# Attention and highway layer on one core: the last sum of the highway layer and the doubling of x on GpSimd in place of VectorE

## The chip, the cores and the metric

One core of one Trainium2 chip runs the whole kernel. The metric is the device time of one execution in microseconds (us); a lower figure is better.

Names of engines: PE is TensorE's matmul, PEld its weight load, DVE is VectorE, ACT is ScalarE, POOL is GpSimd, SP is SyncE.

## The reference

Sliding-window attention (window 128, plus 4 sink keys) over 4 batches, 8 heads, 768 positions, head size 64, then a highway layer over the 3072 tokens with 512 features:

```python
def _attn_ref(q, k, v, n_sink, window):
    scores = scale * np.matmul(q, k.transpose(0, 1, 3, 2))
    scores = np.where(is_sink | in_window, scores, -1e9)
    a = np.exp(scores - scores.max(-1, keepdims=True))
    a = a / (a.sum(-1, keepdims=True) + 1e-09)
    return np.matmul(a, v)
# x = attention's output as [3072, 512]
def _moe_ref(x, w_h, w_t, b_t):
    H = np.maximum(x @ w_h, 0.0)
    T = 1.0 / (1.0 + np.exp(-(x @ w_t + b_t)))
    return T * H + (1.0 - T) * x
```

## The kernel before

The kernel works on 24 tiles of 128 tokens, six per batch (c = 0 to 5). It keeps half of x (xh = x/2) in fp16, so that the gate is T = (1 + tanh)/2 and the output is 2·xh + (1 + u)·dd with u = tanh and dd = max(hps, 0) − xh, where hps is half of x·w_h. The order on PE, DVE and ACT is the program order; GpSimd's order is chosen by the scheduler. All loads of q, k and v are issued by GpSimd, which is busy for about 0.9 us with each (914 ns for q, 916 for k).

```python
    td_pool = ctx.enter_context(tc.tile_pool(name="p_td", bufs=3))     # u, dd, ee
    m_ps = ctx.enter_context(tc.tile_pool(name="ps_m", bufs=2, space=bass.MemoryType.PSUM))
    # ... (cut)
    def stage_T(n):                       # transposes of q and k, for tile n
        tp = m_ps.tile([P, 2 * NHP, P], FP16, tag="m", name="tp")
        # ... 8 transposes on PE (cut)
        nc.scalar.copy(out=qT, in_=tp[:, 0:NHP, :])
        nc.vector.tensor_copy(out=kT, in_=tp[:, NHP:2 * NHP, :])

    def stage_mask(n):                    # two masks a tile; both inputs are in SBUF
        for e in es:
            nc.vector.tensor_tensor(out=ev, in0=ev,
                in1=m.unsqueeze(1).to_broadcast([P, 4, np_ * P]), op=ALU.mult)

    # stage_A ends with rec = 1/sum and xh = av * rec (av is in PSUM), on VectorE
    # stage_sink_setup (once a batch) has two small copies on VectorE (ks), then vs, the sinks' values:
            nc.vector.tensor_copy(out=ks3[rows, :, 4 * hh:4 * hh + NSINK],
                                  in_=kT[rows, :, 0:NSINK])

    def stage_Mh(n):
        # ... 4 matmuls into hps (cut)
        dd = td_pool.tile([P, DM], FP16, tag="dd", name="dd")
        nc.vector.scalar_tensor_tensor(out=dd, in0=hps, scalar=0.0, in1=xh,
                                       op0=ALU.max, op1=ALU.subtract)
        ee = td_pool.tile([P, DM], FP16, tag="ee", name="ee")
        nc.vector.scalar_tensor_tensor(out=ee, in0=u, scalar=1.0, in1=dd,
                                       op0=ALU.add, op1=ALU.mult)
        otok = o_pool.tile([P, DM], FP32, tag="otok", name="otok")
        nc.vector.scalar_tensor_tensor(out=otok, in0=xh, scalar=2.0, in1=ee,
                                       op0=ALU.mult, op1=ALU.add)
        nc.sync.dma_start(out=out[n * P:(n + 1) * P, :], in_=otok)

    with tc.manual_schedule(engines={ENG.PE, ENG.DVE, ENG.Activation}):
        for i in range(-2, NB + 1):
            # load(i+4); sink(i); S(i+1); A(i); T(i+2); mask(i+1); Mt(i-1); X(i); sink setup; Mh(i-1)
```

The softmax here doesn't subtract the row's maximum and nothing guards it: scores larger than these inputs give would overflow.

## Time and profile before

| | kernel before |
|---|---|
| time, median | 144.44 us (144.27 to 144.75) |
| span of the profiled run | 143.0 us |
| six tiles (one batch) in the steady part | 29.1 us |
| from hps to hps: tile with sink scores, without, c = 0, sink setup, the one after it | 5.00, 4.55, 4.50, 5.47, 4.60 us |

The last row is worked out from the start times of the first hps matmul of each tile in the timeline.

Lines of the page of the kernel before. The first is the busy time of each engine, its share of the span and its instructions; the second is the chain of waits that ended last; the others are groups: line, engine, operation, output and inputs with their shapes, count, busy us and mean ns of one, then the idle time before them.

```profile
PE 114.4 (80%) x1312; PEld 73.8 (52%) x1312; DVE 114.1 (80%) x228; ACT 90.3 (63%) x129; POOL 66.8 (47%) x86
...
DVE 36%; PE 32%; ACT 10%; DMA 7%; issue 7%; POOL 6%; DVEq 0%; POOLq 0%
...
L247 DVE TENSOR_TENSOR e<-e,mask 128x1024 f16<-128x1024 f16 x32 | 20.5, 682 | 0.0
...
L316 DVE SCALAR_TENSOR_TENSOR ee<-u,dd 128x512 f16<-128x512 f16 x24 | 16.6, 692 | 2.9 <-ACT es L214 0.5
...
L319 DVE SCALAR_TENSOR_TENSOR otok<-xh,ee 128x512 f32<-128x512 f16 x24 | 16.6, 692 | 0.8
```

VectorE and TensorE are equally busy, and VectorE leads the chain, so an operation taken off VectorE looks like a gain. But the chain alternates between the engines, and one tile of the timeline shows why. Columns: start, duration, engine, line, operation; in brackets the idle time before it and what ended it.

```profile
60.19 0.69 DVE L319 SCALAR_TENSOR_TENSOR otok<-xh,ee 128x512 f32<-128x512 f16 x1
...
60.80 0.20 DVE L275 RECIPROCAL rec<-av 128x8 f32<-128x8 f32 x1
...
61.04 0.69 DVE L277 TENSOR_TENSOR xh<-av,rec 128x512 f16<-128x512 f32 x1
...
61.50 0.58 ACT L176 COPY qT<-tp 128x512 f16<-128x512 f16 x1
...
62.12 0.42 DVE L177 COPY kT<-tp 128x512 f16<-128x512 f16 x1 [0.39 <-ACT qT L176]
...
62.46 1.28 DVE L247 TENSOR_TENSOR e<-e,mask 128x1024 f16<-128x1024 f16 x2
62.60 1.02 PE L310 MATMUL hps<-wh_sb,xT 128*128 128x512 f16 x4
...
63.66 0.69 DVE L313 SCALAR_TENSOR_TENSOR dd<-hps,xh 128x512 f16<-128x512 f32 x1
...
64.46 0.69 DVE L316 SCALAR_TENSOR_TENSOR ee<-u,dd 128x512 f16<-128x512 f16 x1
```

VectorE is ready for kT at 61.73 but waits 0.39 us for ScalarE's qT, and hps starts right after kT. An earlier xh would not have moved this hps. In this kernel "VectorE is 80% busy" and "VectorE's work sets the time" are different statements.

### The profile page before, as it was taken

Reading aid. Unit: us, or ns where it says so; the run is one execution under the profiler, and the core shown is the slowest. Engines: PE = TensorE matmul, PEld = TensorE weight load, DVE = VectorE, ACT = ScalarE, POOL = GpSimd, SP = SyncE. Lnnn points to the kernel's source line nnn. Section 1 sums busy time; section 2 is a strip of 40 time slices with the busy share of each in tenths; the row PEclk is TensorE's granted clock in tenths of the full one; section 3 lists DMA queues with packets and bytes.
Section 4 is the critical chain, followed back from the end, with each engine's and each line's share of the span. In section 5 each row is a group of like instructions: output and inputs, shape, how many; then the busy total and the mean of one; then the engine's idle time right before and its main releaser. Section 6 shows DMA issues by size and latency. Waiting matters only on the chain.

```text
span 143.0 us, 3308 instructions
## 1 busy us (share of the span) xinstructions
PE 114.4 (80%) x1312; PEld 73.8 (52%) x1312; DVE 114.1 (80%) x228; ACT 90.3 (63%) x129; POOL 66.8 (47%) x86
## 2 busy tenths in 40 slices
PE   0345046999999969999999699999997999999730
PEld 0134034775676525756765366567644656675310
DVE  6825007588989899989898999899889998999690
ACT  3056026187787677779766867887759579774310
POOL 6999569719975744376349424753040000000000
PEclk9999999999999999999999999999999999999996
DMA  1999999999999998999999999999869021011111
GB/s 10 112 126 156 161 155 155 155 112 142 150 179 201 163 181 64 155 153 137 131 153 125 160 100 135 146 138 134 113 101 124 0 78 73 14 64 73 73 73 73
DMA packets 79408, 16.98 MB, mean 119 GB/s; under 512 B 75297, under 2 KB 76321, under 8 KB 79394
## 3 DMA queue, kind: packets, MB, share of 16 engines
q0 software_dynamic: 75936, 10.49, 109.1%
q1 hardware_dynamic: 3458, 6.30, 12.7%
q8 instruction: 10, 0.16, 0.4%
q14 instruction: 4, 0.03, 0.1%
HBM read 20.97 MB, written 6.29 MB: 191 GB/s over the span
## 4 chain that ended last, share of the span: by engine, by line
DVE 36%; PE 32%; ACT 10%; DMA 7%; issue 7%; POOL 6%; DVEq 0%; POOLq 0%
PE hps L310 12%; DMA ksd<-in_k_dram 7%; DVE ee L316 6%; DVE otok L319 6%; DVE e L247 6%; DVE dd L313 5%; ACT e L234 5%; DVE xh L277 5%; PE av L262 4%; PE tps L298 4%; PE xtp L286 3%; DVE kT L177 3%; PE sk L211 3%; ACT qT L176 2%; DVE vs L196 2%
## 5 line engine op out<-in xcount | busy, mean ns | idle before, releaser
L234 ACT ACTIVATE e<-sps,ebias 128x1024 f16<-128x1024 f32 (+1 forms) x48 | 47.4, 1039 | 15.7 <-PE sps L231 11.4
L298 PE MATMUL tps<-wt_sb,xT 128*128 128x512 f16 x96 | 25.1, 384 | 0.0
L310 PE MATMUL hps<-wh_sb,xT 128*128 128x512 f16 x96 | 24.6, 378 | 0.6
L83 POOL DMA_DIRECT2D qsd<-in_q_dram x24 | 21.9, 914 | 2.7 <-PE tp L173 1.7
L176 ACT COPY qT<-tp 128x512 f16<-128x512 f16 x24 | 14.0, 585 | 14.1 <-PE tp L173 14.1
L84 POOL DMA_DIRECT2D ksd<-in_k_dram x24 | 22.0, 916 | 2.0 <-DMA wh_sb<-in_moe_w_h_dram 2.0
L262 PEld LDWEIGHTS <-e 128*128 128x128 f16 x352 | 20.4, 100 | 4.2 <-DVE vs L196 1.2
L247 DVE TENSOR_TENSOR e<-e,mask 128x1024 f16<-128x1024 f16 x32 | 20.5, 682 | 0.0
L301 ACT ACTIVATE u<-tps 128x512 f16<-128x512 f32 x24 | 14.4, 600 | 9.0 <-PE tps L298 9.0
L177 DVE COPY kT<-tp 128x512 f16<-128x512 f16 x24 | 10.0, 418 | 12.0 <-ACT qT L176 12.0
L313 DVE SCALAR_TENSOR_TENSOR dd<-hps,xh 128x512 f16<-128x512 f32 x24 | 16.5, 687 | 3.4 <-PE hps L310 3.4
L316 DVE SCALAR_TENSOR_TENSOR ee<-u,dd 128x512 f16<-128x512 f16 x24 | 16.6, 692 | 2.9 <-ACT es L214 0.5
L171 PE MATMUL tp<-ident,qsd 128*128 128x128 f16 x96 | 10.2, 234 | 10.6 <-DMA qsd<-in_q_dram 10.6
L231 PE MATMUL sps<-qT,kT 64*128 64x128 f16 x352 | 15.2, 228 | 2.8 <-DVE kT L177 2.1
L319 DVE SCALAR_TENSOR_TENSOR otok<-xh,ee 128x512 f32<-128x512 f16 x24 | 16.6, 692 | 0.8
L277 DVE TENSOR_TENSOR xh<-av,rec 128x512 f16<-128x512 f32 x24 | 16.6, 691 | 0.8
L231 PEld LDWEIGHTS <-kT 64*128 64x128 f16 x352 | 10.7, 99 | 10.1 <-issue 6.8
L288 ACT COPY xT<-xtp 128x512 f16<-128x512 f16 x24 | 14.0, 583 | 1.2 <-PE xtp L286 0.7
L298 PEld LDWEIGHTS <-xT 128*128 128x128 f16 x96 | 9.6, 100 | 9.1 <-issue 0.8
L310 PEld LDWEIGHTS <-xT 128*128 128x128 f16 x96 | 9.2, 97 | 8.1 <-issue 1.3
L171 PEld LDWEIGHTS <-qsd 128*128 128x128 f16 x96 | 7.4, 104 | 11.2 <-DMA qsd<-in_q_dram 10.8
L286 PEld LDWEIGHTS <-xh 128*128 128x128 f16 x96 | 6.2, 100 | 13.1 <-DVE xh L277 11.5
(66 smaller groups left out, 161.8 us busy)
## 6 DMA issues: line engine op xcount, KB each, us to landing
out_dram<-otok SPq DMA_DIRECT2D x24, 256.0 KB, 2.6
qsd<-in_q_dram POOLq DMA_DIRECT2D x24, 128.0 KB, 4.9
ksd<-in_k_dram POOLq DMA_DIRECT2D x24, 128.0 KB, 5.3
v_91<-in_v_dram POOLq DMA_DIRECT2D x4, 128.0 KB, 4.2
v_92<-in_v_dram POOLq DMA_DIRECT2D x4, 128.0 KB, 3.9
wt_sb<-in_moe_w_t_dram POOLq DMA_DIRECT2D x1, 512.0 KB, 7.4
wh_sb<-in_moe_w_h_dram POOLq DMA_DIRECT2D x1, 512.0 KB, 9.5
v_93<-in_v_dram POOLq DMA_DIRECT2D x4, 128.0 KB, 5.3
```

The costliest lines, as they stand in the source:

```text
L83: nc.gpsimd.dma_start(out=qsd, in_=q[b, :, rows, :].transpose([1, 0, 2]))
L84: nc.gpsimd.dma_start(out=ksd, in_=k[b, :, rows, :].transpose([1, 0, 2]))
L231: nc.tensor.matmul(sps[:, hh, o:o + P], lhsT=kk[rows, hp, :], rhs=qT[rows, hp, :], start=True, stop=True)
L234: nc.scalar.activation(out=e.rearrange("p a b c d -> p a (b c d)"), in_=sps[:, :, 0:2 * np_ * P], func=AF.Exp, bias=ebias, scale=SCALE)
L247: nc.vector.tensor_tensor(out=ev, in0=ev, in1=m.unsqueeze(1).to_broadcast([P, 4, np_ * P]), op=ALU.mult)
L262: nc.tensor.matmul(av[:, g, 2 * hl + hh, 0:_AVN], lhsT=es[g][:, hh, hl, pc, :], rhs=vt[:, 65 * h:65 * h + _AVN], start=first, stop=False, ...
L277: nc.vector.tensor_tensor(out=xh, in0=avh[:, :, 0:D], in1=rec.unsqueeze(2).to_broadcast([P, H, D]), op=ALU.mult)
L298: nc.tensor.matmul(tps, lhsT=xT[:, kc, :], rhs=wt_sb[:, kc, :], start=False, stop=(kc == NOC - 1))
L310: nc.tensor.matmul(hps, lhsT=xT[:, kc, :], rhs=wh_sb[:, kc, :], start=(kc == 0), stop=(kc == NOC - 1))
L313: nc.vector.scalar_tensor_tensor(out=dd, in0=hps, scalar=0.0, in1=xh, op0=ALU.max, op1=ALU.subtract)
L316: nc.vector.scalar_tensor_tensor(out=ee, in0=u, scalar=1.0, in1=dd, op0=ALU.add, op1=ALU.mult)
L319: nc.vector.scalar_tensor_tensor(out=otok, in0=xh, scalar=2.0, in1=ee, op0=ALU.mult, op1=ALU.add)
```

## The change

The intent is to take 24 operations of 0.69 us off VectorE and give them to an engine that is 47% busy. GpSimd gets two operations for each one removed: the doubling of xh, which does not depend on the long chain, and the sum. (VectorE's form does both in one operation. A version with that same scalar_tensor_tensor on GpSimd did not compile.)

```diff
     u_of = {}
+    xh2_of = {}
@@ stage_Mh
+        xh2 = td_pool.tile([P, DM], FP16, tag="xh2", name="xh2")
+        nc.gpsimd.tensor_scalar_mul(xh2, xh, 2.0)
+        xh2_of[n] = xh2
         dd = td_pool.tile([P, DM], FP16, tag="dd", name="dd")
@@
         otok = o_pool.tile([P, DM], FP32, tag="otok", name="otok")
-        nc.vector.scalar_tensor_tensor(out=otok, in0=xh, scalar=2.0, in1=ee,
-                                       op0=ALU.mult, op1=ALU.add)
+        nc.gpsimd.tensor_tensor(out=otok, in0=xh2_of.pop(n), in1=ee, op=ALU.add)
         nc.sync.dma_start(out=out[n * P:(n + 1) * P, :], in_=otok)
```

## The prediction

> **What bounds the kernel now.** The page shows PE 80%, DVE 80%, ACT 63%, POOL 47% busy of a 143.0 us span; the chain of waits gives DVE 36% and PE 32%. So DVE looks like the limit. Read in order of time, the steady part (40 to 127 us, 29.1 us per six token tiles) says something narrower. In most tiles two things end together: DVE's otok, rec, xh, and ScalarE's qT copy; kT needs both, and hps waits for kT. From hps start to hps start a tile without sink scores takes 4.55 us, one with them 5.0 us. Both are rebuilt without otok: hps 0.95, (sk 0.46), 0.49 from scores to exponential, two exponentials 2.01, qT 0.62, kT 0.42, 0.06 to hps. In these tiles qT ends between 0.35 us after xh and 0.08 us before it. Only around a batch's first tile (c = 0, half-size exponentials) is DVE clearly late: xh ends 0.57 us after qT, and 0.18 us in the tile after the sink setup.
>
> **Removed, added, moved.** DVE loses 24 otok operations, 692 ns each by record, about 0.61 us by spacing: 15 to 16.6 us of DVE time. POOL gains 24 scalings and 24 sums. Its own memsets (231 ns for 128 elements, 352 for 256) suggest 0.6 us for the scaling. For the sum the Trainium skill, "GPSIMD Engine Reference", section 3.1, gives 4497 ns for 2048 fp32 elements; my estimate for 512 is 1.2 us. No trace here shows either yet. POOL also issues all loads, three of 0.88 us per tile, so its work per tile goes from 2.65 to 4.45 us while loads last (to about 105 us). The instruction order puts each sum between load issues, so POOL will lag. But loads run five to six tiles ahead, and three ee and xh2 buffers allow two tiles of lag: no stall from POOL's throughput.
>
> **Contention.** The Trainium skill, "SBUF — State Buffer", section "Who interferes with whom", says that a DVE instruction with two SBUF inputs contends with a GpSimd instruction that reads SBUF. Here these are the two masks (682 ns each) and ee (692 ns), against both new POOL operations. The trace of before cannot show this. I estimate 0.3 to 0.6 us of DVE delay per tile, which eats most of the 0.61 us freed.
>
> **On the critical path.** Without contention the gain is about 0.75 us per batch boundary (0.45 at c = 0, the rest in the next two tiles), three boundaries: 2.2 us. At the end xh comes 0.7 and dd 0.6 us earlier, but the last sum takes 0.5 us longer and the last hps must still follow: net 0.2 to 0.4 us. Best case about 142. Contention gives back about 1 us.
>
> **Prediction: 143.0 us, range 141.2 to 145.8.** Chances: faster by over 2% 0.09, within 2% 0.84, slower by over 2% 0.07.
>
> **Right or wrong in the profile.** DVE busy falls by 12 us or more (less if masks and ee lengthen); POOL busy rises by 40 us or more; sums near 1.2 us, scalings 0.6 us; hps to hps still 4.55 and 5.0 us in mid-batch tiles; c = 0 tiles 0.4 us shorter; kT waits for ScalarE in nearly all tiles (five in the steady part before); loads issued later but never waited for by transposes.
>
> **What would make it wrong.** If POOL locks DVE out for whole operations more than once a tile, DVE loses over 0.7 us per tile and the kernel is slower by some us. If fp16 sums take 1.6 us or more, POOL lags until ee waits for buffers. If an earlier xh shortens the ScalarE loop too, the gain could reach 4 us.

## More of the kernel before

A pair of full masks, undisturbed, takes 1.28 us in the timeline.

## The result

The changed kernel took 152.49 us (151.46 to 152.95, four runs) against 144.57 us in the same rounds. The ratio is 1.054, with a 95% interval of 1.048 to 1.060: 5.4% slower, and outside the predicted range. Ratios in this document are the mean time of one kernel's fast runs over the mean of the other's fast runs of the same rounds, so they are not quite the ratio of the medians.

The same lines of the page after:

```profile
PE 116.3 (77%) x1312; PEld 74.1 (49%) x1312; DVE 119.1 (79%) x204; ACT 90.8 (60%) x129; POOL 136.1 (90%) x134
...
DVE 43%; PE 21%; ACT 12%; issue 8%; DMA 6%; POOL 6%; POOLq 1%; DVEq 0%; ACTq 0%
...
L247 DVE TENSOR_TENSOR e<-e,mask 128x1024 f16<-128x1024 f16 x32 | 30.7, 1000 | 0.0
...
L320 DVE SCALAR_TENSOR_TENSOR ee<-u,dd 128x512 f16<-128x512 f16 x24 | 20.6, 858 | 3.1
```

VectorE executes 24 instructions fewer and is busy 5.0 us longer. The 16.6 us of otok went, and 21.3 us came back: 13 us on full masks (25.6 to 38.7 us over both groups of them), 2.5 us on the half-size ones, 4.0 us on ee, and about 1.8 us on eight copies of 64x16 elements (ks). (These are sums of durations; the fall and the rise don't add up to 5.0 exactly, since neighbouring records overlap a little.)

Which operations grew is the first clue. Sorting VectorE's records of the changed kernel by whether they overlap a GpSimd doubling or sum:

| VectorE operation | inputs in SBUF | no overlap, us | overlap, us |
|---|---|---|---|
| dd | 1 (hps is in PSUM) | 0.68 (6) | 0.68 (18) |
| xh | 1 (av is in PSUM) | 0.69 (11) | 0.69 (13) |
| kT | 0 (tp is in PSUM) | 0.41 (8) | 0.42 (16) |
| pair of full masks | 2 | 1.32 (2) | 2.00 (14) |
| ee | 2 | 0.76 (5) | 0.88 (19) |

(Mean durations, with the count in brackets; mask pairs with the common mask only; overlaps of 0.01 us or less are left out.) These three operations with no or one SBUF input did not notice GpSimd at all; the ks copies, which have one, are a case of their own, see before_writes. One tile shows the effect at close range, first VectorE's timeline of the changed kernel:

```profile
63.33 0.69 DVE L277 TENSOR_TENSOR xh<-av,rec 128x512 f16<-128x512 f32 x1
64.41 0.42 DVE L177 COPY kT<-tp 128x512 f16<-128x512 f16 x1 [0.39 <-ACT qT L176]
64.75 2.43 DVE L247 TENSOR_TENSOR e<-e,mask 128x1024 f16<-128x1024 f16 x2
67.10 0.68 DVE L317 SCALAR_TENSOR_TENSOR dd<-hps,xh 128x512 f16<-128x512 f32 x1
```

and GpSimd's timeline in the same stretch:

```profile
62.96 1.51 POOL L314 TENSOR_SCALAR xh_935<-xh 128x512 f16<-128x512 f16 x1
64.41 0.94 POOL L84 DMA_DIRECT2D ksd<-in_k_dram  x1
65.36 1.27 POOL L323 TENSOR_TENSOR otok<-xh_843,ee 128x512 f32<-128x512 f16 x1
```

The mask pair took 2.43 us in place of 1.28. The excess, 1.15 us, is the length of an undisturbed sum on GpSimd, and a sum ran from 65.36 to 66.63, inside the pair. Before the sum, GpSimd was issuing a load, and that cost the masks nothing. xh and kT ran past the doubling at full speed.

The doubling is the long one of the two: over its 24 records it takes 1.48 us at least and 1.64 us on average. The sum takes 1.14 us at least and 1.26 on average. With the loads GpSimd is 90% busy, and its two readers run for 2.9 us of a tile of about 5 us. It also runs late: no doubling waits for its xh and only two of the 24 sums wait for their ee, and in the middle of the run a doubling starts up to 14.0 us after the end of its xh, almost three tiles. So both operations run when GpSimd's queue comes to them, and both meet masks: by the records the masks overlap doublings for 12.0 us and sums for 12.4 us.

### The profile page after: what moved, and what is told of

Read it like the earlier page. It is cut to its first block, busy times and chain, and to the rows that moved or that the text cites. A ratio compares the mean times of both kernels' runs of the same rounds, so it can differ in the third digit from the quotient of the medians.

```text
span 150.8 us, 3355 instructions
## 1 busy us (share of the span) xinstructions
PE 116.3 (77%) x1312; PEld 74.1 (49%) x1312; DVE 119.1 (79%) x204; ACT 90.8 (60%) x129; POOL 136.1 (90%) x134
## 4 chain that ended last, share of the span: by engine, by line
DVE 43%; PE 21%; ACT 12%; issue 8%; DMA 6%; POOL 6%; POOLq 1%; DVEq 0%; ACTq 0%
DVE e L247 18%; ACT e L234 8%; PE hps L311 7%; DVE ee L320 7%; DMA ksd<-in_k_dram 6%; DVE xh L277 5%; DVE dd L317 5%; DVE kT L177 4%; PE tps L299 3%; PE av L262 3%; ACT qT L176 3%; DVE vs L196 2%; PE xtp L286 2%; POOL qsd L83 2%; PE sk L211 2%
## 5 line engine op out<-in xcount | busy, mean ns | idle before, releaser
L247 DVE TENSOR_TENSOR e<-e,mask 128x1024 f16<-128x1024 f16 x32 | 30.7, 1000 | 0.0
L262 PEld LDWEIGHTS <-e 128*128 128x128 f16 x352 | 19.9, 100 | 12.0 <-DVE vs L196 5.9
L176 ACT COPY qT<-tp 128x512 f16<-128x512 f16 x24 | 14.1, 586 | 17.9 <-PE tp L173 17.9
L320 DVE SCALAR_TENSOR_TENSOR ee<-u,dd 128x512 f16<-128x512 f16 x24 | 20.6, 858 | 3.1
L277 DVE TENSOR_TENSOR xh<-av,rec 128x512 f16<-128x512 f32 x24 | 16.6, 692 | 0.9
L286 PE MATMUL xtp<-ident,xh 128*128 128x128 f16 x96 | 9.9, 228 | 2.9 <-DVE xh L277 2.6
```

The costliest lines, as they stand in the source:

```text
L247: nc.vector.tensor_tensor(out=ev, in0=ev, in1=m.unsqueeze(1).to_broadcast([P, 4, np_ * P]), op=ALU.mult)
L262: nc.tensor.matmul(av[:, g, 2 * hl + hh, 0:_AVN], lhsT=es[g][:, hh, hl, pc, :], rhs=vt[:, 65 * h:65 * h + _AVN], start=first, stop=False, ...
L277: nc.vector.tensor_tensor(out=xh, in0=avh[:, :, 0:D], in1=rec.unsqueeze(2).to_broadcast([P, H, D]), op=ALU.mult)
L286: nc.tensor.transpose(xtp[:, j, :], xh[:, 2 * j:2 * j + 2, :], ident)
```

## Experiments

Theory A: a GpSimd operation that reads SBUF shuts out VectorE operations with two SBUF inputs while it runs. Theory B: GpSimd is too busy or too far behind, so that results, or the buffers they hold, wait in its queue. Twelve kernels were run.

| run | time, us (median) | kernel before, us | ratio, 95% interval |
|---|---|---|---|
| after | 152.49 | 144.57 | 1.054 (1.048 to 1.060) |
| relief_only (wrong on purpose) | 140.91 | 145.06 | 0.970 (0.964 to 0.977) |
| before_reads | 177.70 | 145.06 | 1.224 (1.216 to 1.231) |
| before_writes | 162.24 | 145.06 | 1.117 (1.108 to 1.126) |
| after_deep | 152.28 | 145.06 | 1.048 (1.040 to 1.056) |
| before_shadow | 162.15 | 145.27 | 1.118 (1.111 to 1.124) |
| writes_shadow | 144.22 | 145.27 | 0.995 (0.990 to 0.999) |
| sum_only (wrong on purpose) | 144.46 | 145.27 | 0.995 (0.991 to 1.000) |
| scale_only | 153.39 | 145.27 | 1.058 (1.053 to 1.064) |
| act_double | 144.41 | 144.74 | 0.998 (0.993 to 1.003) |
| act_double_pinned | 141.57 | 144.74 | 0.980 (0.975 to 0.985) |
| dve_double | 145.26 | 144.74 | 1.003 (0.999 to 1.008) |
| double_by_add | 154.34 | 144.74 | 1.066 (1.061 to 1.072) |

### relief_only: VectorE without the sum, GpSimd unchanged

```diff
-        ee = td_pool.tile([P, DM], FP16, tag="ee", name="ee")
+        ee = o_pool.tile([P, DM], FP32, tag="otok", name="ee")
-        otok = ...   (tile and last sum removed)
-        nc.sync.dma_start(out=out[n * P:(n + 1) * P, :], in_=otok)
+        nc.sync.dma_start(out=out[n * P:(n + 1) * P, :], in_=ee)
```

> The kernel before without its last sum at all; ee is written as fp32 and stored, so the result is wrong on purpose. GpSimd gets no new work. It measures what freeing VectorE of 24 sums is worth by itself. The loop through ScalarE's exponentials, qT, kT and hps (4.55 us and 5.0 us a tile) should stay the limit: 141.5 to 142.5 us, 1 to 2% faster. If VectorE's busy time were the limit, 24 x 0.61 us would go: about 130 us.

It took 140.91 us, 3.0% less, a little more than expected. VectorE's busy time fell from 114.1 to 99.8 us, 14.3 us, and the time by 4.1 us. Its waits say where the rest is (total us, number of waits, the longest):

```profile
DVE kT L177 <- ACT qT L176: 17.0, 20, 6.5
```

kT now waits for qT in 20 of 24 tiles; in the kernel before it did in 9, and for 12.0 us in total. From hps to hps, the steady tiles are 5.00 us with sink scores and 4.55 us without, exactly as before; only the c = 0 tile (4.50 to 4.07 us), the sink setup (5.47 to 5.29) and the one after it (4.60 to 4.55) got shorter, 0.65 us a batch. So about 2 us come from the three batch boundaries. Most of the rest comes from the end: the last ee ended at 135.93 us, where the last otok had ended at 139.58; part of that is simply a last operation that a correct kernel must have somewhere.

### before_reads and before_writes: GpSimd load added to the kernel before

```diff
+        nc.gpsimd.tensor_scalar_mul(sc1, wt_sb[:, 0, :], 2.0)                                      # before_reads
+        nc.gpsimd.tensor_tensor(out=sc2, in0=wt_sb[:, 1, :], in1=wt_sb[:, 2, :], op=ALU.add)       # before_reads
+        nc.gpsimd.memset(sc1, 1.0)      # before_writes, 1472 fp16 elements
+        nc.gpsimd.memset(sc2, 1.0)      # before_writes, 1104 fp16 elements
         dd = td_pool.tile([P, DM], FP16, tag="dd", name="dd")
```

> The kernel before with VectorE unchanged, and GpSimd doing per tile one fp16 scaling and one fp16 sum of constant weights into scratch that nobody reads. Theory A (a GpSimd operation that reads SBUF shuts out VectorE operations with two SBUF inputs): masks from 682 to about 1000 ns, ee and otok from 692 to about 850 ns, dd, xh, kT and rec unchanged, and slower than after because VectorE still does the sum: 155 to 165 us. Theory B (after is slow because results wait in GpSimd's queue behind load issues, or the buffers that they hold): nothing waits for the scratch, VectorE durations stay, 144 to 146 us.

> As before_reads, but the two GpSimd operations are memsets of about the same length (sized for 1.48 and 1.15 us), which only write SBUF. Theory A in the form that only the read side is shared: masks stay at 682 ns, 144 to 146 us. If any GpSimd work in SBUF shuts VectorE out, or if GpSimd's queue being full delays loads, it is slow as before_reads.

before_reads was far slower than either theory said, 177.7 us. Masks went to 960 ns, ee to 812, otok to 1067, and dd, xh and kT stayed, as theory A says. But it also broke something else. The dummy operations depend on nothing that runs late, so they filled GpSimd between the load issues, and PE waited 10.0 us for loads of v, which the kernel before never did. The granted TensorE clock of its runs was lower as well (0.93 to 0.94, against 0.99 to 1.00 in the kernel before). This run supports A but can't give its size.

before_writes missed too: 162.2 us, where theory A with its read side alone said 144 to 146. The masks stayed at 683 ns and ee and otok at 692, so the two-input operations really were untouched. The loss was in the ks copies, one SBUF input each, 64x16 elements. The worst, in VectorE's timeline of before_writes:

```profile
114.97 1.28 DVE L247 TENSOR_TENSOR e<-e,mask 128x1024 f16<-128x1024 f16 x2
116.17 11.26 DVE L187 COPY ks<-kT 64x16 f16<-64x16 f16 x1
```

and GpSimd's timeline under it (the memsets go on without a gap until the copy ends):

```profile
115.94 1.59 POOL L313 MEMSET sc<- 128x1472 f16 x1
117.21 1.29 POOL L315 MEMSET sc<- 128x1104 f16 x1
118.17 1.59 POOL L313 MEMSET sc<- 128x1472 f16 x1
119.44 1.29 POOL L315 MEMSET sc<- 128x1104 f16 x1
```

A copy that takes 0.16 to 0.50 us in the kernel before took 11.26 us; all eight took 17.4 us in place of 1.6. This is a second kind of shutting out: not of two-input operations by reads, but of a single-input fp16 copy from SBUF to SBUF by writes. The Trainium skill, "SBUF — State Buffer", section "Who interferes with whom", names copies among the operations that may use both ports of VectorE and then contend with GpSimd. It says that the loser blocks for the other's whole instruction; here the copy waited for ten in a row, until the last of them had ended at 127.4 us.

### after_deep: theory B's buffers

```diff
-    x_pool = ... bufs=4    td_pool = ... bufs=3    o_pool = ... bufs=4
+    x_pool = ... bufs=9    td_pool = ... bufs=8    o_pool = ... bufs=8
```

> The changed kernel with deeper rings for u, dd, ee, xh2 (3 to 8), xh and xT (4 to 9) and otok (4 to 8). Theory B, buffers held by a lagging GpSimd: recovers most of the loss, 143 to 147 us. Theory A: masks and ee as long as in after, 151 to 154 us.

152.28 us: deeper rings gave nothing. The waits of the changed kernel agree: VectorE's ee never waits for GpSimd, and PE waits for q loads only twice, as before. GpSimd does lag, but results or buffers held in its queue were not what cost time.

### before_shadow and writes_shadow: the same GpSimd work without removing anything

In before_shadow VectorE keeps its sum; GpSimd does the doubling and the sum again, into scratch. Its operations have the same inputs as in the changed kernel, and they fall behind VectorE in a like way (a doubling starts up to 10.4 us after its xh, against 14.0). In writes_shadow they are memsets, and the ks copies are written as a two-input maximum.

```diff
+        nc.gpsimd.tensor_scalar_mul(xh2, xh, 2.0)                            # before_shadow
+        nc.gpsimd.tensor_tensor(out=sc, in0=xh2, in1=ee, op=ALU.add)         # before_shadow
+        nc.gpsimd.memset(sc1, 1.0); nc.gpsimd.memset(sc2, 1.0)               # writes_shadow
         otok = o_pool.tile([P, DM], FP32, tag="otok", name="otok")
@@ stage_sink_setup, writes_shadow only
-            nc.vector.tensor_copy(out=ks3[...], in_=kT[rows, :, 0:NSINK])
+            nc.vector.tensor_tensor(out=ks3[...], in0=kT[rows, :, 0:NSINK],
+                                    in1=kT[rows, :, 0:NSINK], op=ALU.max)
```

> The kernel before, VectorE unchanged and correct, and GpSimd doing the same scaling of xh and the same sum with ee as in after, in nearly the same order, into scratch that is not stored. Theory A (GpSimd reads shut out VectorE's two-input operations): VectorE pays the contention of after and keeps its sum: 155 to 165 us, masks about 1000 ns, ee and otok longer. Theory B (results wait in GpSimd's queue): 144 to 147 us, VectorE durations as before.

> As before_writes, with the eight small ks copies of VectorE written as a maximum of kT with itself (two SBUF inputs, no single-input copy), because they had waited up to 11 us behind memsets there. If only reads of GpSimd shut VectorE's two-input operations out, and the ks copies were the whole loss of before_writes: 144 to 147 us, masks 682 ns. If a busy GpSimd queue by itself costs time: still over 150 us.

Groups of before_shadow:

```profile
L247 DVE TENSOR_TENSOR e<-e,mask 128x1024 f16<-128x1024 f16 x40 | 35.7, 932 | 0.0
L316 DVE SCALAR_TENSOR_TENSOR ee<-u,dd 128x512 f16<-128x512 f16 x24 | 19.8, 826 | 3.5 <-DVE dd L313 0.5
L323 DVE SCALAR_TENSOR_TENSOR otok<-xh,ee 128x512 f32<-128x512 f16 x24 | 19.5, 811 | 0.8
```

Busy times and two groups of writes_shadow:

```profile
PE 114.0 (80%) x1312; PEld 73.6 (52%) x1312; DVE 113.8 (80%) x228; ACT 90.4 (63%) x129; POOL 120.1 (84%) x134
...
L248 DVE TENSOR_TENSOR e<-e,mask 128x1024 f16<-128x1024 f16 x40 | 25.7, 684 | 0.0
...
L320 POOL MEMSET sc<- 128x1472 f16 x24 | 39.6, 1648 | 0.0
```

This pair decides. GpSimd is 87% busy in one and 84% in the other, with the loads interleaved alike. With reads the kernel is 11.8% slower and the masks take 932 ns; with writes it is as fast as the kernel before (0.995) and the masks take 684 ns. Chance of timing doesn't explain it: by the records, 18 of the 20 pairs of full masks overlap a doubling or sum in before_shadow, for 20.5 us in all, and 17 of 20 overlap a memset in writes_shadow, for 17.9 us. The ks copies differ between the two as well, but they took only 4.1 us in one and 1.3 us in the other. GpSimd's being busy costs nothing by itself; its reading does. It also settles before_writes: with the ks copies out of the way, nothing of its loss is left.

### sum_only and scale_only: which of the two operations

```diff
# sum_only: no doubling; the result is wrong
+        nc.gpsimd.tensor_tensor(out=otok, in0=xh, in1=ee, op=ALU.add)
# scale_only: doubling on GpSimd, sum on VectorE
+        nc.vector.tensor_tensor(out=otok, in0=xh2_of.pop(n), in1=ee, op=ALU.add)
```

> GpSimd does only the sum, of xh and ee, without the doubling (wrong on purpose). Theory A: overlap with masks and ee falls with GpSimd's reading time, from about 2.8 to 1.2 us a tile, so over half of the 11.5 us between relief_only and after goes: 142 to 146 us. Masks 750 to 850 ns.

> GpSimd does only the doubling; VectorE adds xh2 and ee (a plain sum of two SBUF inputs, so it can be shut out too). Theory A: VectorE has its sum back and the longer of the two GpSimd readers stays: 149 to 155 us, masks 800 to 900 ns. If the sum on GpSimd were the culprit: 144 to 146 us.

sum_only took 144.46 us, and scale_only 153.39. The doubling alone is as bad as the whole change: with VectorE's 24 sums in place, it adds about 8 us to the kernel before. Masks and doublings of scale_only:

```profile
L247 DVE TENSOR_TENSOR e<-e,mask 128x1024 f16<-128x1024 f16 x40 | 33.5, 877 | 0.0
...
L314 POOL TENSOR_SCALAR xh<-xh 128x512 f16<-128x512 f16 x24 | 36.8, 1534 | 22.7 <-DVE xh L277 22.4
```

The wait at the end of the second line tells why: the doubling starts when VectorE has finished xh, and the masks come on VectorE right after xh and kT. In scale_only 19 of 24 doublings start within 0.6 us of the end of their xh, so they are released into the masks. (In the changed kernel GpSimd is too late for that, see above.) The sum is released by ee, after which VectorE runs rec, xh and kT, none of which has two SBUF inputs. So the sum can be nearly free, if it starts at once. In sum_only it did not always. While GpSimd was catching up with loads, VectorE's timeline of sum_only has

```profile
43.98 2.24 DVE L247 TENSOR_TENSOR e<-e,mask 128x1024 f16<-128x1024 f16 x2
...
68.87 1.28 DVE L247 TENSOR_TENSOR e<-e,mask 128x1024 f16<-128x1024 f16 x2
```

and GpSimd's

```profile
44.16 1.51 POOL L320 TENSOR_TENSOR otok<-xh,ee 128x512 f32<-128x512 f16 x1
...
67.15 1.15 POOL L320 TENSOR_TENSOR otok<-xh,ee 128x512 f32<-128x512 f16 x1 [1.21 <-issue]
```

The late sum at 44.16 falls into a mask pair, and both suffer: the pair takes 2.24 us and the sum 1.51. The prompt sum at 67.15 ends before the next pair and both take their undisturbed times. From 58 us on sum_only keeps relief_only's rhythm (5.00, 4.55, 5.00, 4.07, 5.30, 4.55 us); before that it loses about 1.5 us to lengthened tiles, besides a start that was 1.1 us later (first hps at 29.53 us, in relief_only at 28.45). So sum_only, level with the kernel before, is about 3.5 us behind relief_only by medians of different rounds.

### act_double, act_double_pinned, dve_double: the doubling elsewhere

```diff
# act_double: ScalarE doubles, after its xT copy in stage_X
         nc.scalar.copy(out=xT, in_=xtp)
+        xh2 = x_pool.tile([P, H, D], FP16, tag="xh2", name="xh2")
+        nc.scalar.mul(out=xh2, in_=xh, mul=2.0)
# act_double_pinned: the same, the ks copies as in writes_shadow, and GpSimd in program order
-    with tc.manual_schedule(engines={ENG.PE, ENG.DVE, ENG.Activation}):
+    with tc.manual_schedule(engines={ENG.PE, ENG.DVE, ENG.Activation, ENG.Pool}):
# dve_double: VectorE doubles, in stage_Mh before dd
-        nc.gpsimd.tensor_scalar_mul(xh2, xh, 2.0)
+        nc.vector.tensor_scalar_mul(xh2, xh, 2.0)
```

> A correct form of sum_only: ScalarE doubles x right after its xT copy, in the 0.65 us that it idles there before the next exponentials; GpSimd does only the sum. Theory A: as sum_only, plus up to 0.1 us a tile if ScalarE's gap is too short: 143.5 to 146 us. If a half-free VectorE is all that counts and contention doesn't: as relief_only, 141 us.

> As act_double, with GpSimd kept in program order (each sum ahead of the next tile's loads, so it starts when ee is ready, while VectorE runs rec, xh and kT, which have one SBUF input) and the ks copies as a maximum. Theory A with phase: in sum_only the sums that ran late, behind load issues (39 to 55 us), met the masks and cost about 1.4 us, the later prompt ones nothing; so masks 682 ns nearly everywhere and 141.5 to 144 us. If loads are now too late (issued four tiles ahead at most), transposes wait for DMA and it is slower than act_double.

> VectorE itself doubles x, SBUF to SBUF in fp16 with one input, and GpSimd does only the sum. The ks copies, of the same kind, waited up to 11 us behind GpSimd memsets in before_writes; so these 24 doublings should wait for whatever GpSimd has running or queued: much longer than 0.3 us each, 148 to 165 us. If only two-input operations are shut out: 143 to 145.5 us.

act_double is correct and level with the kernel before. act_double_pinned is correct and takes 141.57 us, 2.0% less than the kernel before and, by medians of different rounds, 11 us less than the changed one. Its interval (0.975 to 0.985) lies below 1 but across the 2% line, so the verdict on record is "unclear" and not "faster". Two of its groups:

```profile
L249 DVE TENSOR_TENSOR e<-e,mask 128x1024 f16<-128x1024 f16 x40 | 25.7, 683 | 0.0
...
L324 POOL TENSOR_TENSOR otok<-xh,ee 128x512 f32<-128x512 f16 x24 | 27.6, 1150 | 38.7 <-DVE ee L321 38.7
```

All 24 sums wait for ee and start at once, not one full mask pair meets a sum, and both are at their undisturbed lengths. One tile on VectorE:

```profile
62.90 0.69 DVE L321 SCALAR_TENSOR_TENSOR ee<-u,dd 128x512 f16<-128x512 f16 x1
63.75 0.21 DVE L277 RECIPROCAL rec<-av 128x8 f32<-128x8 f32 x1 [0.16 <-PE av L270]
63.99 0.69 DVE L279 TENSOR_TENSOR xh<-av,rec 128x512 f16<-128x512 f32 x1
65.10 0.42 DVE L178 COPY kT<-tp 128x512 f16<-128x512 f16 x1 [0.41 <-ACT qT L177]
65.44 1.28 DVE L249 TENSOR_TENSOR e<-e,mask 128x1024 f16<-128x1024 f16 x2
```

and on GpSimd:

```profile
63.67 1.15 POOL L324 TENSOR_TENSOR otok<-xh,ee 128x512 f32<-128x512 f16 x1 [1.23 <-DVE ee L321]
```

The sum runs from 63.67 to 64.82, wholly inside the stretch from ee to the masks. From hps to hps this kernel has 5.01, 4.56, 5.01, 4.07, 5.31 and 4.57 us, relief_only's rhythm to 0.02 us. The doubling on ScalarE, 0.65 us each, fits into a gap. Loads issued four tiles ahead at most were early enough: PE waits for q loads only twice, as before. Two edits were made together here, the order and the ks copies; the four pairs of ks copies fell from about 0.61 to 0.32 us, which points to the order for most of the gain of some 2.8 us over act_double, but the two were not run apart. About half of that gain is the end of contention: act_double loses 1.4 us in two tiles where late sums meet masks (in one of them a ks copy also took 0.61 us beside a load). The other half is an earlier start, with the first hps at 27.48 us in place of 28.98. The kernel before starts it at 28.49, so 1.0 us of the gain over that one is a start that owes nothing to the sum. The kernel before with these two edits alone was not run.

The expectation for dve_double, 148 to 165 us, was wrong: 145.26 us. A doubling on VectorE takes 0.28 us undisturbed. It overlapped a GpSimd sum in only two of 24 tiles (0.67 and 0.29 us). It comes after the masks, when GpSimd is often issuing loads, and these did hold it up at times: seven doublings took 0.39 to 0.71 us, each ending about 0.1 us after the end of a load's issue, while six others beside a load took 0.28 or 0.29 us. That is only 1.4 us in all. So copies like these do wait behind GpSimd's loads, but the waits were short, and sums were hardly tested; timing again decides.

### double_by_add: the doubling as xh + xh on GpSimd

```diff
-        nc.gpsimd.tensor_scalar_mul(xh2, xh, 2.0)
+        nc.gpsimd.tensor_tensor(out=xh2, in0=xh, in1=xh, op=ALU.add)
```

> The changed kernel with the doubling on GpSimd written as xh + xh, a sum like the other (1.15 us undisturbed where the scaling took 1.48). Theory A: a fifth less reading time a tile (2.3 for 2.6 us) takes a fifth or so off the 11.5 us of contention: 149 to 152 us. If the scaling's form, not its time, is what hurts: 145 us or less.

It missed: 154.34 us. (2.3 for 2.6 us is an eighth less, not a fifth, but the measured time lies outside the range by either.) The doublings did shrink to 1.18 us on average, but the full masks grew further, to 1112 ns. One tile of 9.79 us in place of 4.61 accounts for about 5 us of loss: there a pair of ks copies took 2.75 us, PE waited 3.3 us for vs behind them, and the next mask pair took 2.61 us. In the same tile the granted TensorE clock fell (0.50 from 60 to 64 us of the profiled run). The two runs with a mean clock of 0.967 took 155.28 and 154.72 us, the two at 0.991 took 153.65 and 153.96, so about 1 us of the loss in the former may be the clock. Less reading time did not bring a gain, and less overlap did not either: by the records the full masks overlapped GpSimd's two operations for 18.6 us here and 21.8 us in the changed kernel, yet lengthened by 17.2 us here and 13.0 there. Why is not known.

## Why the prediction was wrong

**What held.** The reading that VectorE's busy time does not set the time was right. relief_only shows hps to hps unchanged at 4.55 and 5.00 us in mid-batch tiles, and the c = 0 tile shorter by 0.43 us, where 0.45 was predicted. The boundary gain was 0.65 us a batch, predicted 0.75. The sum was estimated at 1.2 us from the Trainium skill, "GPSIMD Engine Reference", section 3.1, and took 1.15 undisturbed, with fp16 inputs: the trace agrees. "No stall from POOL's throughput" held as well: after_deep gained nothing, and loads, issued later, were never waited for after the start.

**The mechanism was named.** The prediction said that masks and ee would contend with GpSimd's reads, and cited the Trainium skill, "SBUF — State Buffer", section "Who interferes with whom". The trace agrees: masks from 682 to 1000 ns, ee from 692 to 858, dd, xh and kT unchanged, and before_shadow against writes_shadow (masks 932 against 684 ns) shows reads to be the cause.

**The step that failed is its size**: "I estimate 0.3 to 0.6 us of DVE delay per tile, which eats most of the 0.61 us freed." Measured, VectorE's lengthened operations cost 21.3 us over 24 tiles, 0.89 us a tile, more than the 0.61 freed. VectorE's busy time, predicted to fall by 12 us or more, rose by 5.0. "Contention gives back about 1 us" was really about 11.6 us, the changed kernel's 152.49 less relief_only's 140.91 (different rounds; it includes a first hps that starts 1.3 us later, and the last sum, which relief_only leaves out). The waits show how the delay reached the time. PE's av needs the masked e and vs. In the kernel before it waited for them once, at the start. The lines give total us, number of waits and the longest, first of the kernel before, then of the changed one:

```profile
PE av L262 <- DVE vs L196: 1.0, 1, 1.0
...
PE av L262 <- DVE vs L196: 5.2, 4, 1.8
PE av L262 <- DVE e L247: 2.1, 5, 0.9
```

Three terms in that size were wrong:

- The doubling. "Its own memsets suggest 0.6 us for the scaling" was 1.48 us undisturbed and 1.64 on average. It took a memset of 1472 elements to run about as long (1.46 us on average in before_writes). GpSimd's reading time a tile was 2.9 us rather than 1.8.
- The overlap. By the records masks and ee overlapped the two GpSimd operations for 36.2 us, 1.5 us a tile, and lengthened by 19.5 us, about half of that. Two masks and ee are 2.06 us of a tile of 4.85; if they met the prediction's own 1.8 us of reading by chance, the overlap would be about 0.76 us a tile, and 1.2 us with the measured 2.9 us in a tile of 5.1 (estimates from these durations). So the overlap was about double what those figures give, mostly because of the longer reading. That POOL would lag was predicted, but not that the sums would then fall on the masks: sum_only, whose sums mostly started at once, was level with the kernel before, while scale_only, with the doubling alone, was 5.8% slower.
- The ks copies. The prediction named "the two masks" and ee; the eight ks copies were held up too (about 1.8 us), right ahead of vs, for which PE waited.

The prediction did list this outcome ("If POOL locks DVE out for whole operations more than once a tile, DVE loses over 0.7 us per tile and the kernel is slower by some us"), but gave it a chance of 7%.

**Left open.** Not every length fits the rule of one blocked operation: a mask pair at 99.56 us of the changed kernel took 3.03 us, an excess of 1.75, with only about 0.9 us of a sum and 0.4 us of a doubling under it. Nor does every overlap cost: eight of the 19 ee that overlap by the records kept their 0.69 us, and one of 1.04 us has only loads beside it. How the two engines hand over was not measured.

## What to carry to other kernels

Before moving elementwise work to GpSimd, list the VectorE operations with two SBUF inputs (and the SBUF-to-SBUF copies), and look at what VectorE runs at the moment when the moved operation is released, not at how busy either engine is. Here one sum a tile on GpSimd was free when it started on time against one-input operations, and the doubling alone, released into the masks, cost about 8 us, twice what taking the sum off VectorE could gain (4 us). Check too whether the helping engine keeps up: when GpSimd fell behind, its prompt operations became late ones. Measure first what freeing the engine is worth by deleting the work: it put a ceiling of about 3% on this change.

## What the Trainium skill lacked or had wrong

- "GPSIMD Engine Reference", section 4.1 calls one-input elementwise work roughly line-rate. A one-input fp16 multiplication by a constant of 128x512 elements took 1.48 us undisturbed, longer than a two-input sum of the same size (1.15 us), whose estimate from section 3.1 (1.2 us) was good.
- "SBUF — State Buffer", section "Who interferes with whom", says that the loser blocks for the other's whole instruction. A 64x16 fp16 copy on VectorE waited 11.26 us, through ten GpSimd memsets that followed each other without a gap. The page does not warn that the wait can last over many instructions.
- No page says what a given amount of overlap costs a pair of back-to-back VectorE operations; the runs show an excess from nothing to 1.75 us on a pair of 1.28 us.
